# ScalarE's scores ahead of VectorE's in each step of an attention kernel, and one more zero matmul

## The chip, the core and the metric

The kernel runs on one core of a Trainium2 chip. The metric is the device time of one execution in microseconds (us). Five engines work side by side, each through its own instruction queue in program order: TensorE (PE in the profile, its weight loads PEld), VectorE (DVE), ScalarE (ACT), GpSimd (POOL) and SyncE (SP), which issues most of the DMAs.

## What is computed

The input x is 2048 tokens of 448 features. Two branches are mixed by a gate per token:

```python
g = _sigmoid((x * gate_w).sum(-1, keepdims=True))
a = _A_ref(x, A_wqkv, A_wo)      # 16 heads of 28: softmax(q k^T / sqrt(28)) v, then wo
b = _B_ref(x, B_w_r, B_w_i)      # rfft2 of x, times w_r + i w_i, irfft2
return g * a + (1 - g) * b
```

What matters here is the attention: for each of 16 heads a 2048 by 2048 matrix of scores, the exponential of every score, and the product of these with v.

## The kernel before

**Slices and chunks.** The heads stand in 4 groups of 4. Group T keeps its four heads in the four 32-row strips of the tiles `qT` and `kT`: head h of a group lies in rows 32h to 32h+31. A score matmul (`score`, L818 to L822) contracts the 32 rows of one strip and gives a slice of 128 keys by 512 queries, one PSUM bank. Matmuls on different strips of the array can run side by side. The work is cut into 16 chunks (a group and 512 queries), and a chunk into 16 blocks of 128 keys by 4 heads, so 64 slices a chunk and 1024 in all.

**Two engines make the exponentials.** ScalarE takes slices in order, in tiles of three and two by turns: `ps3` (3 banks) and `ps2` (2 banks), one buffer each. The pass that turns one tile into bf16 is the exponential at L1053; it writes `Pt` (and, near the start, the borrowed tiles `early`, `oT` and `CR`). VectorE takes whole blocks, called packs: each of the four slices of a pack has its score written to one of two spare PSUM banks, `bg0` and `bg1`, from where the instruction at L834 takes it to the tile `Pd`. After the fourth, a chain of six or seven VectorE instructions (L849 to L883) makes the exponentials, for most packs with an accumulating DMA on GpSimd's queue (L878) as the last step. The 1024 slices divide into 892 for ScalarE and 132 for VectorE.

**TensorE's other work.** The matmuls with v (L974, on 32-column strips, into the bank `psPV`), the projections for the next group (L280, L493), and the stages of the Fourier branch (L660 to L754) and of the output (L769, L773). These run in units of one to four phases, which also write `bg0` and `bg1` and are emptied by VectorE. Beside them there are matmuls on the zero tile `warm`, whose results are not used or add nothing: on all 128 rows at L1249, L991 and L1255, and on a single 32-row strip at L1010.

**The order is fixed while the program is built.** `stream` (L1288 to L1352) walks through step k = 0, 1, 2, ... of ScalarE's tiles. It keeps model clocks (`tp` for TensorE, `tv` for VectorE, `ta` for ScalarE) and constants of cost, and from these it picks which units fit in the step. One step emits the exponential of tile k, up to two or three matmul groups with v, units as long as they fit, zero matmuls where the last steps hold too few columns (`dummy`), zero matmuls while TensorE would stand idle until ScalarE is done (`until`, L1268), and then, in `scores(k + 2, end)`, what is needed for tile k + 2. The scores of tile k + 2 go to the buffer that tile k used, so on the chip they wait until the exponential of tile k has ended.

**`scores`** (L977 to L1000) is where the change lies. It first tries `away` (L1015): if a `bg` bank is free by the model and VectorE is not too far behind, the next slice of a pack is scored there, on a strip that the tile of ScalarE doesn't use where the pack has such a slice left, else on one that it does. `away` also puts the VectorE instruction of L834 into VectorE's queue, and up to some of its waiting chain before it. If `away` emits nothing, `zeros` (L1002) puts one zero matmul on a strip that the tile of ScalarE doesn't use, if a `bg` bank is free by the model. After either of these come the two or three scores of ScalarE's tile. All of these are in TensorE's one queue, so whatever stands first there holds up what stands behind it. The pack's score and the zero matmul wait for VectorE to have emptied their bank; ScalarE's scores wait for ScalarE to have emptied `ps`.

Of the kernel before, what the change touches and what calls it, by code (L numbers as in the profile page):

```python
# [43 lines left out]
E_SC, E_EX, E_PV, E_PV2, E_MM = 0.32, 0.05, 0.33, 0.215, 0.22  # L44
# [12 lines left out]
FIRST = 3  # L57
SOON = 18.1
STEPS, THIN = 3400, 3300
NV, NBASE = 10, 12  # L60
MOST = 7
LATE, LATE_END = 4, 5
# [10 lines left out]
def with_free(ap, free):  # L73

    return _AP(tensor=ap.tensor, offset=ap.offset, ap=[list(ap.ap[0])] + [list(x) for x in free])
# [77 lines left out]
class Kernel:  # L153
# [740 lines left out]
    def fill_v(self, until, most=1000):  # L894
        while self.vq and self.tv < until and most:
            fn, cost, of = self.vq.pop(0)
            self.dve(cost, True, of=of)
            most -= 1
            fn()
# [77 lines left out]
    def scores(self, k, end):  # L977

        if self.act_c >= NC or not self.next_tile(k):
            return False  # L980
        t = self.tiles[k]
        for c, i, _ in t:
            if c < 4:
                self.tp = max(self.tp, self.marks[f"q0.{c}"], self.marks[f"k0.{i // 4}"])
        start = max(self.tp, end + AP)
        if not self.away(start, [h for _, _, h in t]) and k > 1:
            self.zeros(start, [h for _, _, h in t])
        n = 2 if k % 2 else 3
        ps = self.psp.tile([P, n, QW], F32, name=f"ps{n}", tag=f"ps{n}", bufs=1)
        for _ in range(self.owed):  # L990
            self.nc.tensor.matmul(ps[:, 0, :], lhsT=self.warm[:], rhs=with_free(self.warm[:], [[0, 4], [1, P]]), start=True, stop=True)  # L991
        self.owed = 0
        for e, (c, i, h) in enumerate(t):
            self.score(ps[:, e, :], c, i, h)
        self.ring[k] = ps
        start = max(self.tp, end + AP)
        self.tp = start + E_SC
        self.add(self.tp, 128 * len(t))
        self.sc[k] = start + 0.50
        return True  # L1000
# [266 lines left out]

    def until(self, at):  # L1268

        while self.tp + E_MM <= at and self.thin(at) and self.one_zero():  # L1270
            self.tp += E_MM
        self.tp = max(self.tp, at)

# [258 lines left out]
```

## Time and profile before

| what | value |
|---|---|
| median of 3 runs | 426.84 us (426.67 to 428.08) |
| the profiled execution's own time | 426.82 us |
| its span, first instruction to last | 425.0 us |
| granted TensorE clock | 1.0 |
| exponentials of ScalarE (L1053) | 357: 178 of three slices, 179 of two; the first starts at 9.15 us, the last ends at 417.07 us |
| pack scores (L820 into `bg`) | 132 |
| zero matmuls on one strip (L1010) | 92 |

The busy share of the engines in the span is 96% for TensorE, 93% for VectorE, 97% for ScalarE and 12% for GpSimd. The busy time of TensorE says little by itself: matmuls are pipelined, and the profile models their ends. A timeline gives the start of each group of equal instructions, the time from its first start to its last end, the engine, the line, and in brackets the idle time of the engine before it with what ended it. A window view gives the busy time of each engine in a stretch of the span.

### The profile page before, as it was taken

What the parts mean: (1) busy time and instruction counts of PE and PEld (TensorE: products, weight loads), DVE (VectorE), ACT (ScalarE), POOL (GpSimd) and SP (SyncE); (2) the same over time, 40 slices, a digit from 0 to 9 for tenths busy, and PEclk for the clock granted to TensorE, in tenths of its full rate; (3) what the DMA queues carried; (4) which work ended last, traced back from release to release, by engine and by line L of the source; (5) the groups of instructions that cost most, each with busy time, mean ns of one, the idle gap of its engine ahead of it and who ended that gap; (6) DMA issues with size and microseconds to landing.
All of it is one profiled execution on the core that took longest, in us unless ns stands there. A gap on an engine that the chain in (4) does not pass through costs nothing.

```text
span 425.0 us, 8196 instructions
## 1 busy us (share of the span) xinstructions
PE 408.4 (96%) x3139; PEld 144.9 (34%) x3139; DVE 395.3 (93%) x643; ACT 411.0 (97%) x369; POOL 50.3 (12%) x57
## 2 busy tenths in 40 slices
PE   9999999999999999999999999999999899999996
PEld 5343233333333333333333333333343233222331
DVE  6669889999989999999999999999999999999996
ACT  4999999999999999999999999999999999999994
POOL 6000002020110112011220100102002011201000
PEclk9999999999999999999999999999999999999999
DMA  9900200232302153375664446526453305240242
GB/s 242 211 11 2 7 27 13 64 60 43 77 15 47 24 97 62 74 166 103 159 148 95 104 103 134 96 68 110 108 149 77 76 2 106 54 107 29 57 99 75
DMA packets 30967, 35.08 MB, mean 83 GB/s; under 512 B 13296, under 2 KB 23536, under 8 KB 30896
## 3 DMA queue, kind: packets, MB, share of 16 engines
q1 hardware_dynamic: 26432, 20.48, 20.4%
q0 software_dynamic: 3744, 13.63, 17.5%
q8 instruction: 24, 0.39, 0.4%
q10 hardware_dynamic: 752, 0.44, 0.4%
q14 instruction: 15, 0.12, 0.1%
HBM read 15.10 MB, written 1.96 MB: 40 GB/s over the span
## 4 chain that ended last, share of the span: by engine, by line
PE 45%; ACT 25%; DVE 22%; issue 7%; ACTq 0%; DVEq 0%
ACT Pt L1053 21%; PE psPV L974 8%; PE ps L820 7%; DVE Pd L834 5%; PE bg L820 4%; PE psPV L1255 3%; PE bg L280 3%; PE bg L1010 3%; DVE pa L875 2%; PE bg L769 2%; PE bg L773 2%; DVE n L849 2%; DVE Pd L852 2%; DVE pa L861 2%; ACT early L1053 2%
## 5 line engine op out<-in xcount | busy, mean ns | idle before, releaser
L1053 ACT ACTIVATE Pt<-ps 128x1536 bf16<-128x1536 f32 x339 | 385.9, 1305 | 1.5 <-PE ps L820 0.6
L820 PE MATMUL ps<-qT,kT 32*128 32x512 bf16 x892 | 143.2, 382 | 4.3 <-ACT Pt L1053 2.8
L834 DVE TENSOR_SCALAR Pd<-bg 128x512 uint16<-128x512 f32 x132 | 90.0, 682 | 6.0 <-PE ps L820 4.2
L974 PE MATMUL psPV<-Pt,vsb 128*32 128x512 bf16 x832 | 81.1, 388 | 0.0
L820 PEld LDWEIGHTS <-kT 32*128 32x128 bf16 x1024 | 44.7, 91 | 95.1 <-issue 90.0
L820 PE MATMUL bg<-qT,kT 32*128 32x512 bf16 x132 | 50.6, 383 | 0.8 <-DVE Pd L834 0.3
L878 POOL DMA_DIRECT2D Pd<-pa x26 | 24.0, 924 | 214.7 <-PE ps L820 108.8
L1255 PE MATMUL psPV<-warm 128*128 128x512 bf16 x129 | 41.5, 385 | 0.0
L875 DVE TENSOR_TENSOR pa<-pa,n 128x2048 uint16<-128x2048 f16 (+1 forms) x33 | 40.9, 1240 | 0.5
L861 DVE TENSOR_TENSOR pa<-pa,n 128x2048 f16<-128x2048 f16 x33 | 40.9, 1239 | 0.3
L974 PEld LDWEIGHTS <-vsb 128*32 128x32 bf16 x1024 | 23.4, 93 | 52.0 <-issue 51.5
L1010 PE MATMUL bg<-warm 32*128 32x512 bf16 x92 | 35.2, 383 | 1.9 <-DVE Pd L834 1.8
L963 POOL TENSOR_TENSOR oT<-o,rep 128x512 bf16<-128x512 f32 x14 | 17.7, 1264 | 144.5 <-DVE oT L962 77.3
L280 PE MATMUL bg<-xT,Wg 128*128 128x512 bf16 (+1 forms) x112 | 29.6, 381 | 0.4
L852 DVE TENSOR_SCALAR Pd<-Pd 128x2048 uint16<-128x2048 uint16 x33 | 24.9, 755 | 0.3
L849 DVE TENSOR_SCALAR n<-Pd 128x2048 uint16<-128x2048 uint16 x33 | 22.9, 693 | 0.5
L864 DVE TENSOR_SCALAR pa<-pa 128x2048 f16<-128x2048 f16 x33 | 23.0, 698 | 0.0
L857 DVE TENSOR_SCALAR pa<-n 128x2048 f16<-128x2048 uint16 x33 | 22.5, 682 | 0.0
L671 DVE CAST U<-bg 128x450 bf16<-128x450 f32 x32 | 19.9, 621 | 2.0 <-PE bg L683 1.2
L1010 PEld LDWEIGHTS <-warm 32*128 32x128 bf16 x92 | 8.3, 91 | 28.8 <-issue 28.1
L769 PE MATMUL bg<-Binv,VT 128*128 128x448 bf16 x64 | 16.4, 355 | 0.1
L1255 PEld LDWEIGHTS <-warm 128*128 128x128 bf16 x131 | 9.5, 97 | 19.5 <-issue 17.9
(183 smaller groups left out, 430.0 us busy)
## 6 DMA issues: line engine op xcount, KB each, us to landing
Pd<-pa POOLq DMA_DIRECT2D x26, 512.0 KB, 4.8
rep<-rD SPq DMA_DIRECT2D x56, 64.0 KB
CR<-cRB SPq DMA_DIRECT2D x8, 256.0 KB
UT<-U SPq DMA_DIRECT2D x16, 112.5 KB
VT<-U SPq DMA_DIRECT2D x16, 112.5 KB
CR<-cCS SPq DMA_DIRECT2D x8, 192.0 KB
xtok<-in_A_x_dram SPq DMA_DIRECT2D x3, 448.0 KB
out_dram<-fin SPq DMA_DIRECT2D x12, 112.0 KB
```

What stands on the lines that cost most here:

```text
L280: self.nc.tensor.matmul(ps[:], lhsT=self.Wg[T, q][0:k, c, :], rhs=self.xT[0:k, c, 512 * b:512 * b + 512], start=(c == 0), stop=(c == 3))
L769: nc.tensor.matmul(ps[:, 0:D], lhsT=self.VT[:, t, 128 * (2 * fb + r):128 * (2 * fb + r) + 128], rhs=self.Binv[:, fb, r, :], start=(fb == 0 ...
L820: self.nc.tensor.matmul(out, lhsT=self.kT[T][32 * h:32 * h + 32, 128 * i:128 * i + 128], rhs=self.qT[T][32 * h:32 * h + 32, QW * qc:QW * q ...
L834: nc.vector.tensor_scalar(out=pk["t"][:, h, :], in0=ps[:], scalar1=SCALE * LOG2E * 512.0, scalar2=127.0 * 512.0, op0=ALU.mult, op1=ALU.add)
L849: v.tensor_scalar(out=st["n"][:], in0=t[:], scalar1=511, scalar2=None, op0=ALU.bitwise_and)
L852: v.tensor_scalar(out=t[:], in0=t[:], scalar1=127 << 9, scalar2=2, op0=ALU.bitwise_and, op1=ALU.logical_shift_right)
L861: v.tensor_tensor(out=st["a"][:], in0=st["a"][:], in1=st["n"][:], op=ALU.mult)
L875: v.tensor_tensor(out=q, in0=st["a"][:], in1=st["n"][:], op=ALU.mult)
L974: self.nc.tensor.matmul(self.psPV[32 * h:32 * h + 32, :], lhsT=self.vsb[:, i, 4 * T + h, :], rhs=pcs[h], start=first, stop=last, tile_posi ...
L1010: self.nc.tensor.matmul(ps[:], lhsT=self.warm[sl], rhs=with_free(self.warm[sl], [[0, 4], [1, P]]), start=True, stop=True, tile_position=(3 ...
L1053: self.nc.scalar.activation(out=Pt[:, 0:n, :], in_=ps[:, 0:n, :], func=ACT.Exp, scale=SCALE)
L1255: self.nc.tensor.matmul(self.psPV[:], lhsT=self.warm[:], rhs=with_free(self.warm[:], [[0, 4], [1, P]]), start=False, stop=False, skip_grou ...
```

## The change

In `scores` the two lines that call `away` and `zeros` move behind the loop that emits ScalarE's scores. In `until` a zero matmul is also let through where the idle time ahead is longer than 0.9 us by the model and the columns in the model's window are below 3900.

```diff
@@ constants
 STEPS, THIN = 3400, 3300
+
+LONG, FULL = .9, 3900
@@ scores
         start = max(self.tp, end + AP)
-        if not self.away(start, [h for _, _, h in t]) and k > 1:
-            self.zeros(start, [h for _, _, h in t])
         n = 2 if k % 2 else 3
         ps = self.psp.tile([P, n, QW], F32, name=f"ps{n}", tag=f"ps{n}", bufs=1)
...
         for e, (c, i, h) in enumerate(t):
             self.score(ps[:, e, :], c, i, h)
         self.ring[k] = ps
+
+        if not self.away(start, [h for _, _, h in t]) and k > 1:
+            self.zeros(start, [h for _, _, h in t])
         start = max(self.tp, end + AP)
@@ until
-        while self.tp + E_MM <= at and self.thin(at) and self.one_zero():
+        long = at - self.tp > LONG
+        while self.tp + E_MM <= at and (self.thin(at) or long and self.activity(at) < FULL) and self.one_zero():
             self.tp += E_MM
```

In the built programs the instruction orders of VectorE, ScalarE, GpSimd and SyncE are the same in both. TensorE's differs in 224 places, at each of which a pack's score or a one-strip zero matmul goes from directly in front of ScalarE's scores to directly behind them (132 packs, 92 zero matmuls), and in one more zero matmul of L1255 (in front of the scores of step 288, around 337 us of the trace of before), and another of these zero matmuls that stood in front of the scores of step 290 and stands behind them.

## The prediction

> **What bounds the kernel now.** I read the groups by line first, then busy time in stretches, then the timeline of single steps. The page's costliest group is ScalarE's exponential:
>
> ```profile
> L1053 ACT ACTIVATE Pt<-ps 128x1536 bf16<-128x1536 f32 x339 | 385.9, 1305 | 1.5 <-PE ps L820 0.6
> ```
>
> In the stretch from 157 us to the last exponential's end ScalarE is busy 259.44 of 260.07 us, VectorE 252.01:
>
> ```profile
> 157.00:417.07 260.07, 253.03 (x1921) 87.27 (x1919) 252.01 (x391) 259.44 (x229) 33.20 (x32) 1.00 0.45 95
> ```
>
> So ScalarE ends the stream and almost never stands idle by this count. It does lose time: in the timeline an exponential of three slices is usually followed by the next start after 1.330 us, one of two after 0.903. 178 and 179 of these make 398.4 us, while the first start (9.15) to the last end (417.07) is 407.9. Of the 9.5 between, 57 exponentials that start over 0.02 us late hold 8.4. That is all a change of this kind can win. TensorE decides the rest, and two places beside each other show how. In both a pack's score (bg) starts with ScalarE's two scores (ps):
>
> ```profile
> 370.86 0.37 PE L820 MATMUL bg<-qT,kT 32*128 32x512 bf16 x1
> 370.86 0.39 PE L820 MATMUL ps<-qT,kT 32*128 32x512 bf16 x2
> ...
> 373.28 0.39 PE L820 MATMUL bg<-qT,kT 32*128 32x512 bf16 x1
> 373.28 0.59 PE L820 MATMUL ps<-qT,kT 32*128 32x512 bf16 x2
> ```
>
> At 370.86 the pack has a strip of its own and all three run together (0.39). At 373.28 it holds the strip of one of ScalarE's scores, which starts about 0.22 us later (0.59 until the last end). ScalarE notices, with its exponential at 373.98:
>
> ```profile
> 373.98 2.37 ACT L1053 ACTIVATE Pt<-ps 128x1024 bf16<-128x1024 f32 x2 [0.20 <-PE ps L820]
> ```
>
> It starts 0.37 us later than the one before allows. But most late starts have another cause: TensorE comes late from the units (in 226 of 355 steps the scores start over 60 ns after their buffer is free, at 52 ns where only the buffer was awaited). The change doesn't shorten the units.
>
> **The change, part by part.** I went through all 224 moved places in the timeline, noting for each the start of the moved matmul and of the scores, shared strips, ScalarE's lateness and VectorE's start.
>
> *1. Shared strip, pack no longer in front.* 29 packs share a strip with the tile (by the strips in the built program). In 11 of these steps ScalarE is late, by 0.09 to 0.37 us. Taking in each the smaller of its lateness and the 0.17 to 0.22 us of spread gives 1.65 us.
>
> *2. Release.* The extra matmul in front also delays ScalarE's release where it has its own strip: the exponential starts 0.132 to 0.139 us after the modelled end of the last score, against 0.098 to 0.107 where nothing stood in front. An example of each, pack in front (scores end 141.97, ScalarE 142.10) and none (397.59, 397.69):
>
> ```profile
> 141.58 0.38 PE L820 MATMUL bg<-qT,kT 32*128 32x512 bf16 x1
> 141.59 0.39 PE L820 MATMUL ps<-qT,kT 32*128 32x512 bf16 x2
> ...
> 142.10 1.02 ACT L1053 ACTIVATE Pt<-ps 128x1024 bf16<-128x1024 f32 x1 [0.17 <-PE ps L820]
> ```
>
> 27 late steps times 0.031 us is 0.8. [...]
>
> *3. Bank wait.* Where the moved matmul waits for VectorE while `ps` is free, it holds the scores. Steps at 44.8, 255.7, 338.3, 371.4, 406.8 and 16.7 us are late and lose 0.03 to 0.12 to it: 0.3. The longest wait (1.06 us before the zero matmul at 337.77) costs almost nothing, because `ps` came free only 0.11 before it ended.
>
> That is 2.75 gross. **What is given back.** In these steps what TensorE does next starts no earlier: it stands behind the moved matmul. An exponential on time thus meets later scores that are where they were. At 176.97 the shared strip cost 0.096; the scores of the next exponential had 0.057 in hand, so 0.039 goes back. At 190.55 0.12 is won, and the scores after next (192.91) were 0.115 late anyway, so all of it goes. Followed from step to step until TensorE next waits for ScalarE, 1.4 of the 2.75 stays.
>
> *4. Packs that ran ahead.* 86 of the moved matmuls started over 12 ns before the scores, 16.3 us in all, while TensorE waited for ScalarE. With a strip of their own they now run beside the scores for some ns. On a shared strip they come 0.22 after, and so does all that follows on TensorE:
>
> ```profile
> 157.74 0.38 PE L820 MATMUL bg<-qT,kT 32*128 32x512 bf16 x1
> 158.11 0.39 PE L820 MATMUL ps<-qT,kT 32*128 32x512 bf16 x3
> 158.44 1.04 PE L280 MATMUL bg<-xT,Wg 128*128 128x512 bf16 x4
> ```
>
> Here L280 would start 0.21 later. 16 such places make 2.3 us of TensorE's time. Most is swallowed by TensorE's next wait (the zero matmul after 87.0 had 0.26 of it). About 0.4 reaches an exponential, at 162.4, 293.1 and 371.4, and 0.5 more goes because TensorE's later steps no longer have room for what 1 to 3 won. So 0.9 lost; bounds 0 and 2.3.
>
> *5. VectorE.* It must wait where the new start of a pack's score is later than the time it now has in hand. For 113 of 132 it isn't: the score has mostly been done 0.3 us or more when VectorE comes. For 19 it is, 2.1 us in sum; the largest are 0.59 (the pack above: 0.37 of lead and 0.22 of strip), 0.28 at 42.6, and 0.22 to 0.24 at 87.0, 176.3 and 358.1. VectorE's idle time covers these: 0.80 us at 43.0, 0.14 at 91.0, 0.28 at 165.2, 0.38 at 359.6. I take 0; bounds 0 and 2.1. It can't be below nothing, since no pack's score starts earlier. Without that cover it reaches TensorE through the banks: 20% of 306 bank changes start 52 to 57 ns after VectorE's last read, so they wait for VectorE.
>
> *6. The zero matmul.* It falls into the 1.06 us before 337.77 where TensorE stands idle, and needs some 0.22 us and a change of shape of about 0.1: 0. The one that goes behind step 290's scores takes 0.22 out of their way, but they had 0.12 in hand: 0. No other queue is passed: no DMA moves, and the other four orders are the same.
>
> **Sum.** 426.8 - 2.75 + 1.35 + 0.9 = 426.3 us, the profiled execution's own 426.82 being the median of 426.84 within its spread. A change below 0.3% (1.3 us) can't be told from none here, so this is "no change".
>
> **Rivals.** *Late steps clear:* the gains of 1 to 3 aren't given back, and TensorE finds its idle time after part 4. Then -1.4 to -2.75: 424.1 to 425.4, say 424.9. For it: 129 of 355 steps do wait for ScalarE, so a gain can stay. Against it: the worked places above.
>
> *VectorE becomes the bound (slower):* its 2.1 us are not made good. It has only 8 us idle in the 260 from 157 on, and an L834 that waits holds up the chain and the unit copies queued behind it, whose banks TensorE awaits. It decides where VectorE's lateness exceeds its idle time up to the next bank that TensorE awaits: the 0.59 of 157.74 meets 0.28 of idle time at 165.2, and at 167.53 a unit takes its bank only 0.11 after VectorE freed it, so some 0.25 passes. If the like happened at all 19 places, the gain were lost and 2.1 came on top: 428.4 to 428.9. Against it: early places meet larger gaps.
>
> [...]
>
> That the change doesn't do what it says is out: the built order shows all 224 swaps.
>
> **How the numbers follow.** Forecast (within 0.3%) 0.53; late steps clear, by over 0.3%, 0.31; VectorE 0.12 and clock 0.04, slower by over 0.3%, together 0.16. The range, 424.9 to 428.3, takes in most of the first rival and the lower half of VectorE's case, and with them the bounds of parts 4 and 5 nearly to their ends.
>
> **What would show it.** Right: no exponential behind a spread of 0.59 or 0.60 in `ps`; the release at 0.10 to 0.11 us everywhere; packs on shared strips 0.22 behind the scores; the late starts falling from 8.4 us to about 7.9; VectorE's wait at L834 up from 6.0 to at most 8. Wrong: late starts below 7 us (first rival); new waits of TensorE for L834 or for unit copies, and `psPV` matmuls waiting for `Pd` (second); a clock below 1.00 (third). The prediction falls too if the matmul behind the scores holds up units by waiting for its bank, which before shows only five times.

## The result, and the profile after

The changed kernel takes 428.44 us (median of 20 runs, 428.02 to 429.79), the kernel before 427.30 beside it (20 runs, 426.62 to 429.38). The ratio is 1.0026, with an interval from 1.0017 to 1.0036: **slower by 0.26%**, about 1.1 us. That is less than 0.3%, as forecast, but on the other side of no change, and above the range's end of 428.3. The profiled execution of the changed kernel took 428.76 us, 1.9 more than that of before, and its span grew by 2.0.

The page of the changed kernel has these groups. The columns are the line and the instruction, the count, then the busy time in us and the mean ns of one, then the idle time of the engine just ahead of it and what ended most of that:

```profile
L1056 ACT ACTIVATE Pt<-ps 128x1536 bf16<-128x1536 f32 x339 | 386.6, 1302 | 1.9 <-PE pv L976 0.7
L822 PE MATMUL ps<-qT,kT 32*128 32x512 bf16 x892 | 139.6, 383 | 14.1 <-ACT Pt L1056 10.9
L836 DVE TENSOR_SCALAR Pd<-bg 128x512 uint16<-128x512 f32 x132 | 90.4, 685 | 7.0 <-PE bg L822 6.5
...
L1013 PE MATMUL bg<-warm 32*128 32x512 bf16 x92 | 35.3, 384 | 0.0
```

The same scores and the same VectorE instruction on the page of before:

```profile
L820 PE MATMUL ps<-qT,kT 32*128 32x512 bf16 x892 | 143.2, 382 | 4.3 <-ACT Pt L1053 2.8
L834 DVE TENSOR_SCALAR Pd<-bg 128x512 uint16<-128x512 f32 x132 | 90.0, 682 | 6.0 <-PE ps L820 4.2
```

The exponential itself is unchanged (1302 ns against 1305). TensorE now stands 14.1 us idle ahead of the scores instead of 4.3, mostly waiting for ScalarE. (On the page of before 0.8 and 1.9 us more stand ahead of the packs' scores and of the zero matmuls.) That looks like more room, but it is the time in which the moved matmuls used to run: they filled the wait for `ps`, and now come after it. VectorE waits 1.0 us more at its first instruction.

The stretch from 157 us to the last exponential's end (us, then the busy time of PE, PEld, DVE, ACT and POOL with counts, the granted clock, the DMA share and GB/s):

```profile
157.00:418.98 261.98, 249.18 (x1925) 86.43 (x1931) 253.59 (x392) 261.29 (x231) 33.45 (x32) 1.00 0.44 94
```

The last exponential ends 1.91 us later than before (418.98 against 417.07); 0.14 of it is there when the first one starts (9.29 against 9.15). Counted as in the prediction, exponentials that start over 0.02 us late are 63 with 10.05 us, where 57 had 8.39: 1.66 more. The tail behind the last exponential is 8.0 us in both. So the loss is in the late starts, at a granted clock of 1.00.

**The gains that were promised did come.** The place that stood at 373.28 with a spread of 0.59 is now this, in TensorE's timeline of the changed kernel:

```profile
375.12 0.39 PE L822 MATMUL ps<-qT,kT 32*128 32x512 bf16 x2
375.35 0.37 PE L822 MATMUL bg<-qT,kT 32*128 32x512 bf16 x1
375.65 0.55 PE L775 MATMUL bg<-Wo,oT 128*128 128x448 bf16 x2
```

The two scores of ScalarE run together, the pack starts 0.23 behind, and the exponential is late by 0.034 us instead of 0.367. The next unit pays, as the prediction said: it starts 0.53 us after the scores, where it takes 0.32 if nothing stands between. And the place of 141.58, with the pack on a strip of its own:

```profile
142.87 0.39 PE L822 MATMUL ps<-qT,kT 32*128 32x512 bf16 x2
142.88 0.38 PE L822 MATMUL bg<-qT,kT 32*128 32x512 bf16 x1
...
143.36 1.02 ACT L1056 ACTIVATE Pt<-ps 128x1024 bf16<-128x1024 f32 x1 [0.23 <-PE bg L822]
```

The scores end at 143.26 and ScalarE starts 0.10 later, not 0.13. (The bracket names `bg` because its update lies nearest; the program's wait is for the scores.)

**What came with them was not in the prediction.** Take a zero matmul with a unit behind it, first before, then after, in TensorE's timeline:

```profile
270.85 0.38 PE L1010 MATMUL bg<-warm 32*128 32x512 bf16 x1
270.86 0.39 PE L820 MATMUL ps<-qT,kT 32*128 32x512 bf16 x2
271.29 0.35 PE L694 MATMUL bg<-UT,E 128*128 128x450 bf16 x1
```

```profile
272.46 0.39 PE L822 MATMUL ps<-qT,kT 32*128 32x512 bf16 x2
272.47 0.38 PE L1013 MATMUL bg<-warm 32*128 32x512 bf16 x1
272.95 0.35 PE L696 MATMUL bg<-UT,E 128*128 128x450 bf16 x1
```

Read the starts against each other: from the first score to the unit it was 0.43 us, and is 0.49. Where the zero matmul had run ahead, the step is larger. Before:

```profile
66.76 0.37 PE L1010 MATMUL bg<-warm 32*128 32x512 bf16 x1
67.00 0.39 PE L820 MATMUL ps<-qT,kT 32*128 32x512 bf16 x3
67.33 1.04 PE L280 MATMUL bg<-xT,Wg 128*128 128x512 bf16 x4
...
68.30 0.39 PE L820 MATMUL ps<-qT,kT 32*128 32x512 bf16 x2
68.74 0.73 PE L493 MATMUL bg<-Wqkv,xT 128*128 128x336 bf16 x4
69.40 0.39 PE L820 MATMUL ps<-qT,kT 32*128 32x512 bf16 x3
```

After:

```profile
67.95 0.39 PE L822 MATMUL ps<-qT,kT 32*128 32x512 bf16 x3 [0.30 <-ACT Pt L1056]
67.97 0.39 PE L1013 MATMUL bg<-warm 32*128 32x512 bf16 x1
68.44 1.02 PE L282 MATMUL bg<-xT,Wg 128*128 128x512 bf16 x4
69.40 0.39 PE L822 MATMUL ps<-qT,kT 32*128 32x512 bf16 x2
...
69.88 0.73 PE L495 MATMUL bg<-Wqkv,xT 128*128 128x336 bf16 x4
70.55 0.39 PE L822 MATMUL ps<-qT,kT 32*128 32x512 bf16 x3
```

From the first scores to the unit 0.33 has become 0.49. One step on there is another such place (0.44, now 0.48), and the scores two steps on come 2.60 us behind the first ones instead of 2.40. The built order of TensorE, with its waits, says why:

```
L1013 Matmult bg_3954<-warm 128x512 [waits DVE_49]
L696  Ldweights E_136
L696  Matmult bg_3958<-UT,E_136 128x450 [waits PE_49]
```

The unit waits for TensorE's own semaphore. `zeros` writes a spare bank but doesn't mark it as taken in the planner (`bank_free` stays), so the next unit often picks the same bank and must wait until the zero matmul has written it. 31 of the 92 zero matmuls are followed by such a unit. No list of waits shows it: TensorE counts as busy while the matmul that it waits for is running, and the rest, some 0.1 us from that matmul's end (272.47 and 0.38) to the unit's start, has no bracket in the timeline. Only the starts show it.

### The profile page after: what moved, and what is told of

The parts are those of the page before. It is cut to its first block, busy times and chain, and to the rows that moved or that the text cites. A ratio compares the mean times of both kernels' runs of the same rounds, so it can differ in the third digit from the quotient of the medians.

```text
span 427.0 us, 8179 instructions
## 1 busy us (share of the span) xinstructions
PE 399.5 (94%) x3121; PEld 143.5 (34%) x3140; DVE 396.2 (93%) x643; ACT 412.0 (96%) x369; POOL 50.5 (12%) x57
## 4 chain that ended last, share of the span: by engine, by line
ACT 46%; PE 28%; issue 13%; DVE 9%; DMA 2%; SPq 0%; DVEq 0%; ACTq 0%
ACT Pt L1056 45%; PE ps L822 8%; PE psPV L976 5%; PE bg L282 2%; DVE Pd L836 2%; DMA xtok<-in_A_x_dram 2%; PE bg L771 2%; PE bg L775 2%; PE bg L495 1%; DVE pa L877 1%; PE psPV L1258 1%; ACT early L1056 1%; PE bg L662 1%; PE bg L822 1%; PE bg L755 1%
## 5 line engine op out<-in xcount | busy, mean ns | idle before, releaser
L1056 ACT ACTIVATE Pt<-ps 128x1536 bf16<-128x1536 f32 x339 | 386.6, 1302 | 1.9 <-PE pv L976 0.7
L822 PE MATMUL ps<-qT,kT 32*128 32x512 bf16 x892 | 139.6, 383 | 14.1 <-ACT Pt L1056 10.9
L822 PEld LDWEIGHTS <-kT 32*128 32x128 bf16 x1024 | 42.5, 91 | 121.2 <-issue 117.4
L282 PE MATMUL bg<-xT,Wg 128*128 128x512 bf16 (+1 forms) x93 | 28.1, 380 | 1.9 <-DVE Pd L836 0.2
L662 PE MATMUL bg<-Bd,xT 128*128 128x450 bf16 x64 | 15.6, 355 | 0.8 <-DVE Pd L836 0.4
```

Of the source, the lines that this page charges most:

```text
L282: self.nc.tensor.matmul(ps[:], lhsT=self.Wg[T, q][0:k, c, :], rhs=self.xT[0:k, c, 512 * b:512 * b + 512], start=(c == 0), stop=(c == 3))
L822: self.nc.tensor.matmul(out, lhsT=self.kT[T][32 * h:32 * h + 32, 128 * i:128 * i + 128], rhs=self.qT[T][32 * h:32 * h + 32, QW * qc:QW * q ...
L1056: self.nc.scalar.activation(out=Pt[:, 0:n, :], in_=ps[:, 0:n, :], func=ACT.Exp, scale=SCALE)
```

## The experiments

Three theories stood against each other. **A, the own bank:** the 31 zero matmuls whose bank the next unit takes hold that unit up, and more so behind the scores. **B, the shared strip:** the 29 packs that come 0.22 us behind the scores make what follows late. **C, VectorE:** the packs come too late for VectorE, which then frees its banks late. The extra zero matmul of `until` was a fourth suspect.

In every kernel the orders of the other four engines stayed those of before; only TensorE's queue differs. The kernels were run in four sets, each on one chip with the kernel before beside it: e1 to e4, e5 to e8, e9 to e12, and e13 with e14. Three sums were taken from each trace. Call the step from ScalarE's first score to TensorE's next work a hand-over. *Own wait*: the hand-overs less 0.32 us each, where that next work waits for TensorE's own semaphore. *Other*: the same where it doesn't; this is a rough sum, since waits for VectorE and ScalarE are in it and the longest hand-overs, of over about 1 us, are not. Over the hand-overs that wait for nothing alone it is 4.1 us before, 7.0 in the changed kernel, 5.4 in e6, 6.1 in e9, 4.6 in e10 and 4.1 in e8 and e11. *Late*: the late starts of the exponentials.

| kernel | own wait, us | other, us | late, us | time against before, with its 95% interval |
|---|---|---|---|---|
| before | 2.46 (21 waits) | 8.48 | 8.39 | 1 |
| after | 5.25 (31) | 12.90 | 10.05 | 1.0026 [1.0017, 1.0036] |
| e1 | 2.44 (21) | 12.54 | 11.14 | 1.0014 [0.9994, 1.0033] |
| e2 | 5.24 (31) | 9.22 | 10.27 | 1.0035 [1.0023, 1.0048] |
| e3 | 5.25 (31) | 12.63 | 9.44 | 1.0030 [1.0019, 1.0041] |
| e4 | 0 | 12.72 | 7.52 | 1.0001 [0.9984, 1.0017] |
| e5 | 6.03 (32) | 11.54 | 10.56 | 1.0024 [1.0014, 1.0034] |
| e6 | 5.27 (31) | 10.21 | 9.54 | 1.0032 [1.0012, 1.0052] |
| e7 | 0 | 9.90 | 7.58 | 0.9967 [0.9955, 0.9979] |
| e8 | 0 | 8.75 | 8.36 | 0.9970 [0.9959, 0.9982] |
| e9 | 0 | 11.95 | 8.94 | 0.9987 [0.9978, 0.9996] |
| e10 | 0 | 9.92 | 7.87 | 0.9988 [0.9979, 0.9996] |
| e11 | 0 | 8.67 | 7.53 | 0.9990 [0.9979, 1.0000] |
| e12 | 0 | 12.76 | 7.52 | 0.9986 [0.9977, 0.9996] |
| e13 | 2.44 (21) | 12.95 | 8.41 | 1.0007 [0.9991, 1.0022] |
| e14 | 10.45 (30) | 12.88 | 13.20 | 1.0125 [1.0105, 1.0144] |

**e1: only the packs behind**, the zero matmuls in front as before. `would` makes the tests of `away` and gives the strip of the next slice (or None), without emitting.

```diff
-        if not self.away(start, [h for _, _, h in t]) and k > 1:
-            self.zeros(start, [h for _, _, h in t])
+        strips = [h for _, _, h in t]
+        pk = self.would(start, strips) is not None
+        if not pk and k > 1:
+            self.zeros(start, strips)
...
         self.ring[k] = ps
+        if pk:
+            self.away(start, strips)
```

> Only the 132 pack scores go behind ScalarE's scores; the 92 one-strip zero matmuls stay in front and the extra zero matmul is left out. Theory A (the zero matmul behind the scores makes the next unit, which takes the same bank, wait for it): no slower than before, ratio 0.998 to 1.001, since the 31 such waits keep their old length (0.12 us or none). Theory B (packs on a shared strip, 0.21 us behind the scores, push TensorE's next work): this carries the whole loss, ratio 1.002 to 1.004. Theory C (VectorE late): as B, and the waits at L834 rise by 1 us or more and TensorE waits more for L834.

1.0014, between the ranges of A and of B, with an interval from 0.9994 to 1.0033. VectorE's idle time at its first instruction is 7.13 us, all that the changed kernel has (7.01). So the packs' move brings most of what B and C speak of. Whether it carries a part of the loss this run alone doesn't say; e9 and e12 below do. The late starts of its trace can't be set against the others: that execution has a stretch at a lower clock (a mean of 0.57 from 304 to 308 us), told of at the end.

**e2: only the zero matmuls behind.**

```diff
+        pk = self.would(start, strips) is not None
+        if pk:
+            self.away(start, strips)
...
         self.ring[k] = ps
+        if not pk and k > 1:
+            self.zeros(start, strips)
```

> Only the 92 one-strip zero matmuls go behind ScalarE's scores; the packs stay in front and the extra zero matmul is left out. Theory A: slower than before, ratio 1.001 to 1.004, with about 30 steps in which the next unit starts 0.48 us after the scores instead of 0.32 to 0.44. Theories B and C: ratio 0.999 to 1.001, a little faster if anything, from the earlier release of some 15 late exponentials (0.03 us each).

1.0035: the whole loss, with the packs where they were. VectorE's idle time is 5.96, as before, and the own wait is that of the changed kernel. This is against B and C.

**e3: the changed kernel without the extra zero matmul.**

```diff
-        while self.tp + E_MM <= at and (self.thin(at) or long and self.activity(at) < FULL) and self.one_zero():
+        while self.tp + E_MM <= at and self.thin(at) and self.one_zero():
```

> The changed kernel without its extra zero matmul. All of A, B and C: as the changed kernel, ratio 1.0017 to 1.0036. If the extra zero matmul (theory D) makes the loss: ratio 0.998 to 1.001.

1.0030 beside the 1.0026 of the changed kernel, and the intervals overlap. The extra matmul isn't the cause.

**e4 and its repeat e12: the changed kernel without the 31.** `SKIP` holds the numbers of the 31 zero matmuls whose bank the next unit takes; the planner's account is kept, so the rest of the order stays. The output doesn't change.

```diff
+            n = self.nz = getattr(self, "nz", -1) + 1
+            if n in SKIP:
+                self.add(start, 128)
+                return
             ps = self.psp.tile([P, 512], F32, name=f"bg{b[0]}", tag=f"bg{b[0]}", bufs=1)
```

> The changed kernel without the 31 one-strip zero matmuls whose bank the next unit takes; nothing else moves. The output is as before, a zero matmul adds nothing. Theory A: 31 times 0.16 us of TensorE's time come back (5 us gross), of which a third may reach ScalarE: 1 to 2 us faster than the changed kernel, ratio to before 0.997 to 1.000. Theories B and C: as the changed kernel, ratio 1.0015 to 1.0035. [...]

> The changed kernel without the 31 once more, beside its relatives: all packs and the other 61 zero matmuls behind. If only the shared packs make the difference: within 0.2 us of the run with all packs behind and zero matmuls in front, and 0.3 to 1 us slower than the base of this call.

1.0001 and 0.9986: the loss is gone, with all packs behind. Beside e3, in the same set, e4 is 1.35 us faster (medians 428.16 and 426.81). The place of 272.46, in e12:

```profile
272.64 0.39 PE L823 MATMUL ps<-qT,kT 32*128 32x512 bf16 x2
272.96 0.36 PE L697 MATMUL bg<-UT,E 128*128 128x450 bf16 x1
```

The unit comes 0.32 us after the scores.

**e5: the changed kernel without the other 61**, which no unit waits for. The same edit, with the other numbers in `SKIP`.

> The counterpart of the run without the 31: here the other 61 one-strip zero matmuls are left out of the changed kernel, and the 31 whose bank the next unit takes stay. Theory A (the wait for the zero matmul's own bank): no gain, ratio 1.002 to 1.004, as the changed kernel. If any matmul behind the scores cost time, taking out 61 would bring more than taking out 31 did: ratio below 1.000. [...]

1.0024. Taking out twice as many of the same matmuls brings nothing. It is not the zero matmul as work for TensorE that costs, but the wait of the unit behind it.

**e6: the changed kernel with the 29 packs on shared strips back in front.**

```diff
+        h0 = self.would(start, strips)
+        first = h0 in strips
+        if first:
+            self.away(start, strips)
...
-        if not self.away(start, [h for _, _, h in t]) and k > 1:
-            self.zeros(start, [h for _, _, h in t])
+        if h0 is not None and not first:
+            self.away(start, strips)
+        if h0 is None and k > 1:
+            self.zeros(start, strips)
```

> The changed kernel with only the 29 packs that share a strip put back in front of ScalarE's scores; packs with a strip of their own and all zero matmuls stay behind. Theory B (shared packs push TensorE's next work by 0.21 us, which costs more than the 0.2 us won for the 11 late exponentials): faster than the changed kernel by 0.3 to 1 us, ratio to before 1.000 to 1.002. If the shared packs behind were a gain in sum: slower than the changed kernel, ratio 1.003 to 1.005.

1.0032. The other hand-overs fall by 2.69 us (12.90 to 10.21), 1.5 of it at those that wait for nothing, VectorE's idle time is down to 6.43, and the time doesn't follow. That is against B. The interval is wide, since two of the executions took 431.8 us at a clock of 0.988, but by the medians (428.25 against 427.34) the loss is there too, and e9 and e12 test B again.

**e7: e6 without the 31** (both edits, e6 and e4). **e8 and its repeat e11: the kernel before without the 31** (the edit of e4 alone).

> Both remedies: no zero matmul of the 31, and the 29 shared packs in front. If A and B each take their part: 0.3 to 1 us faster than with the first remedy alone, ratio 0.998 to 0.9995. If B is nothing: as with the first remedy alone, 0.999 to 1.001.

> The kernel before, without the 31 zero matmuls whose bank the next unit takes; nothing moves. Theory A holds before too, where 21 next units wait 0.12 us each (2.5 us of TensorE's time in the trace of before): faster than before by 0.3 to 1 us, ratio 0.9975 to 0.9995. If the wait only matters behind the scores: 0.9995 to 1.0005.

> The kernel before without the 31 zero matmuls once more, as the base of this call: ratio to before 0.996 to 0.998.

0.9967, 0.9970 and 0.9990. The same program gave 0.9970 and 0.9990 in two sets on two chips, the second outside what was expected, so a difference of 0.2% between two sets means nothing here; within a set, e7 and e8 are alike. The 31 cost time in the old order too: by the medians, leaving them out brings 1.05 us in e8 and 0.8 in e11. In the changed order it brings more: 1.35 from e3 to e4 and 2.05 from e6 to e7 (428.25 to 426.20). In the set of e5 to e8, which has both, the difference is 1.0 us, about the loss of the change.

**e9: e8 with all packs behind. e10: e8 with only the 103 packs on a strip of their own behind.** e9 is e1 with the edit of e4. e10 has that edit and this:

```diff
+        h0 = self.would(start, strips)
+        own = h0 is not None and h0 not in strips
+        if h0 is not None and not own:
+            self.away(start, strips)
+        if h0 is None and k > 1:
+            self.zeros(start, strips)
...
         self.ring[k] = ps
+        if own:
+            self.away(start, strips)
```

> The kernel before without the 31 zero matmuls whose bank the next unit takes, and with all 132 packs behind ScalarE's scores (zero matmuls stay in front). Against the run of this call that has no pack moved. Theory B or C (the 29 shared packs behind cost more than they win): 0.3 to 1 us slower than that one. If the pack's place is neutral: within 0.2 us of it.

> As the run before, but only the 103 packs that have a strip of their own go behind; the 29 shared ones stay in front. By the release row (0.03 us for some 15 late exponentials, half of it given back): 0 to 0.4 us faster than the run with no pack moved. If the packs behind cost something even on their own strip (VectorE later, the bank wait in the way of the units): 0.2 to 0.6 us slower.

0.9987 and 0.9988, in one set with e11 (0.9990) and e12 (0.9986): four kernels within 0.04%. The medians lie further apart (426.94 for e9, 426.62, 426.37 and 426.29 for e12), but not in the order of the packs: e12 has all of them behind, as e9 has, and is the fastest. So without the 31 it makes no difference that these runs show where the packs stand.

**e13: the changed kernel with only the 31 back in front.**

```diff
+        zf = self.would(start, strips) is None and k > 1
+        if zf and self.nz + 1 in OWN:
+            self.zeros(start, strips)
+            zf = False
...
-        if not self.away(start, [h for _, _, h in t]) and k > 1:
+        if not self.away(start, strips) and zf:
```

> The changed kernel with the 31 zero matmuls whose bank the next unit takes back in front of the scores; all 132 packs, the other 61 zero matmuls and the extra one as in the change. If the place of the 31 carries the loss: the waits fall from 5.2 us to about 2.5 us in the trace and the time to that of before, ratio 0.9985 to 1.0005. If their presence or something else does: as the changed kernel, ratio 1.002 to 1.004.

1.0007. In TensorE's timeline the unit is back at 0.44 us behind the zero matmul that stands first:

```profile
273.35 0.38 PE L1020 MATMUL bg<-warm 32*128 32x512 bf16 x1
273.36 0.39 PE L823 MATMUL ps<-qT,kT 32*128 32x512 bf16 x2
273.79 0.35 PE L697 MATMUL bg<-UT,E 128*128 128x450 bf16 x1
```

**e14: the changed kernel with each of the 31 emitted twice.**

```diff
-            self.nc.tensor.matmul(ps[:], lhsT=self.warm[sl], ...
+            for _ in range(2 if self.nz in OWN else 1):
+                self.nc.tensor.matmul(ps[:], lhsT=self.warm[sl], ...
```

> The changed kernel with each of the 31 zero matmuls emitted twice on the same strip and bank. If the wait for their end is the cost: each next unit starts some 0.21 us later still, 6.6 us more of TensorE's time, and the kernel is 1.5 to 4 us slower than the changed one, ratio to before 1.006 to 1.013. If it is something else that happens once per step: ratio 1.002 to 1.005.

1.0125, in one set with e13. The second matmul has the same strip, and the unit now comes 0.66 us after the scores:

```profile
274.97 0.39 PE L823 MATMUL ps<-qT,kT 32*128 32x512 bf16 x2
274.97 0.60 PE L1016 MATMUL bg<-warm 32*128 32x512 bf16 x2
275.63 0.35 PE L697 MATMUL bg<-UT,E 128*128 128x450 bf16 x1
```

With the packs behind in all of them, the own wait of 0, 2.44, 5.25 and 10.45 us (e12, e13, after, e14) goes with 0.9986, 1.0007, 1.0026 and 1.0125. These stand in several sets, and the two small steps are no larger than what one program differed by between sets, so they don't count by themselves. What counts are the steps within a set: e3 to e4, e6 to e7, and e13 to e14 (medians 427.34 and 431.96, 4.6 us for 8.0 us of own wait; the trace of e14 is of an execution of 433.72). With e2, where the place of the zero matmuls alone was changed, and e5, where the other 61 were left out, A is shown for the loss: it goes with the place, the number and the length of these 31 waits and with nothing else that was tried. A version that keeps the 31 matmuls and gives them another bank was not tried, so it is not shown that another bank would be enough.

What stays open is how B and C share what they cost. The packs' move as a whole comes out at about nothing (e9 and e12 against e11), and e6 against the changed kernel shows no difference either. Where the 31 stand in front, it may cost a little: e1 and e13 lie 0.14% and 0.07% above before, with 1 inside both intervals.

## Why the prediction was wrong

Place by place, 20 exponentials are less late by over 0.03 us, 2.3 us in sum, where the prediction had 2.75. 36 are later, 3.9 us in sum, where it had 2.25 as given back or lost. The gains were sized about right, the losses 1.7 us too low.

**Step 1, shared strip: right.** Of 20 places with a spread over 0.1 us one is left. The four largest late starts fell from 0.335 to 0.114 us (step at 212.5 of before), 0.366 to 0.155 (261.4), 0.259 to 0.051 (305.9) and 0.367 to 0.034 (374.0), 0.97 us of the 1.65 claimed.

**Step 2, release: right.** Late exponentials that only the scores hold up start 0.100 to 0.107 us after the modelled end of the last score nearly everywhere, against up to 0.139 before. The term was a little large: of the late steps, 18 stand at 0.131 to 0.139 before and 10 at 0.113 to 0.122, which makes some 0.7 us and not 0.8.

**Step 3, bank wait: half right.** At 44.8 and 255.7 us 0.109 and 0.083 came back, at 338.3 and 406.8 0.03 each, at 16.7 nothing. At 371.4, claimed as well, the exponential is 0.311 later than it was: ahead of it, in the changed kernel, a unit comes 0.49 behind the scores at 368.84, which is an own wait, and a pack on a shared strip makes the work behind the scores of 371.10 start 0.54 after them. Only waits for VectorE were looked at; TensorE's wait for itself was not.

**Step 4, packs that ran ahead: the mechanism right.** The pack comes 0.22 to 0.23 behind and the next work at 0.53, as it said. e6 puts the 29 shared packs at 2.69 us of TensorE's time, 1.5 of it at hand-overs that wait for nothing; 2.3 was estimated. The three exponentials that it named, at 162.4, 293.1 and 371.4, are later by 0.08, 0.19 and 0.31 us, 0.58 for its 0.4, with the own wait in the last. That "some ns" hold for a strip of its own is right too: where nothing is waited for, the hand-over of such a step has a median of 0.324 us in e10, and 0.321 where nothing stands behind the scores. The 103 packs make it 0.5 us (4.6 in e10 against 4.1 in e11).

**Step 5, VectorE: right.** Its wait rose from 6.0 to 7.0 us, below the limit of 8 that the prediction set, and steps 1 to 5, as far as the packs go, together cost nothing that shows (e9 and e12 against e11). 0.5 us of gain was forecast for all of them.

**Step 6, the zero matmul: right for the added one** (e3). **The step that failed is the sentence in step 4 that took the zero matmuls in with the packs:** "With a strip of their own they now run beside the scores for some ns." For the pack's bank that holds: nobody but VectorE wants it next. For the zero matmul's bank it doesn't, since nothing reserves it, and in 31 of 92 cases the unit behind wants it at once. The term was put at nothing. It measures 2.79 us of TensorE's time (5.25 less 2.46: ten more waits, and 0.169 us each instead of 0.117), of which 0.2 to 0.35% of the time, 0.8 to 1.5 us, reached the end (e2; and e13 to the changed kernel, which goes across two sets).

It was there to be read: 0.43 us at 270.86 of before, beside 0.32 at other hand-overs, in a place where nothing is on record as waiting. The last line of the prediction did name the bank, but as the moved matmul's wait for it, not as a wait of the unit for the moved matmul.

**How it reaches ScalarE.** The place shown at 66.76 of before can be followed. In both kernels its first scores start 0.05 us after `ps` came free, so they are paced by ScalarE. The unit then loses 0.16. The next scores start 0.578 us after their `ps` is free instead of 0.433, those two steps on 0.381 instead of 0.192, and their exponential is late by 0.251 us instead of 0.074. So nearly all of the two own waits arrives. Of 355 steps the scores were paced by ScalarE in 129 before, and are in 108 now.

**The rivals.** *Late steps clear* failed by the sign that the prediction gave it (late starts rose to 10.05 us, not below 7). *VectorE becomes the bound* gave a time near the measured one, 428.4, by a mechanism that isn't there: in e2 VectorE waits no longer than before, and the loss is whole. *The clock*, to which the prediction gave 0.04, is not the loss either: it is granted at 1.00 from 157 us to the last exponential's end in both kernels. No run shows what makes it fall; the one stretch in which a trace has it lower stands in the last section.

## What to carry to other kernels

When a matmul is moved, look not only at what it waits for but at what its output buffer makes the next writer wait for, on its own engine too; read that from starts in the timeline, because TensorE counted as busy here while the matmul that it waited for was running (0.38 us from 272.47, where the unit starts at 272.95). A filler should have a buffer that no neighbour wants next (not tried here), or be left out: the kernels without these 31 fillers ran at 0.9967 to 1.0001 of before, whatever the order of the packs, and are the best found here. And where the gain of a new order is a few tenths of a microsecond in some ten places, each change of 0.1 us at thirty others decides the sign.

## What the runs showed of the hardware

**One execution had about half the clock for some 3.4 us, with no idle gap of over 0.24 us in the 2.56 us ahead.** The profiled execution of e1 was granted a mean clock of 0.57 from 304 to 308 us, and 1.00 from 297 to 304 and from 308 to 315. Here are the stretch (columns as in the window above) and TensorE's matmuls of one kind within and behind it:

```profile
304.00:308.00 4.00, 3.76 (x26) 1.28 (x26) 3.77 (x6) 2.93 (x4) 0.00 (x0) 0.57 0.65 152
```

```profile
304.67 0.42 PE L753 MATMUL bg<-CR,VT 128*113 128x256 bf16 x1
...
308.59 0.27 PE L753 MATMUL bg<-CR,VT 128*113 128x256 bf16 x1
```

The same matmul takes 0.42 us and 0.27. Within the stretch the starts of these and their neighbours of L754 are 0.21 apart (304.46, 304.67, 304.88), behind it 0.10 to 0.11 (308.49, 308.59, 308.70): about half the clock, and by the mean of 0.57 for some 3.4 of the 4 us, an estimate from the two. ScalarE is busy 2.93 of 4.00 us: 1.07 lost. In the 2.56 us ahead of it, from 301.73 to 304.29 us, TensorE's idle gaps were of 0.24 us at most, 0.7 in sum. In the trace of before it was busy 1.51 of the 2.56 us from 335.21 to 337.77, with an idle gap of 1.06, and the clock was 1.00 there and from 337.77 to 341. So of these two places the one with the longer idle time kept its clock.

A lower mean clock isn't rare in these runs. In the set of e1, 10 of 34 executions of the kernel before had a mean clock of 0.993 to 0.995, with a median of 427.52 us against 426.88 of the others: 0.64 us more. In other kernels the difference was larger: 1.3 us in e3 (medians 429.46 and 428.15), and the profiled execution of e1 took 430.51 us, 3.2 more than the median of e1's executions at 0.997 and above. Such executions raise the median of before, whose executions at 0.997 and more have medians of 426.78 to 427.27 us in the four sets. The clocks of the executions beside the changed kernel are not on record; against those four medians, from other sets, it would stand 1.2 to 1.7 us higher, not 1.1. Of the 20 executions of the changed kernel none fell below 0.997, but of e3, which differs from it by one zero matmul, 3 of 12 did, and so did 3 of 12 of e6, which has that matmul. Only e1's stretch was traced; that the others had one is inferred from the mean clock. What sets it off was not settled.
